# A fused attention and two-stage mixture-of-experts kernel: loads, splits and transposes issued at other places, and GpSimd's two splits of 1024 columns in halves of 512

## The chip, the cores and the metric

The kernel runs on one core of one Trainium2 chip. Its time is the device time of one execution in microseconds (us). The engines are PE (TensorE matmul) with its weight loads PEld, DVE (VectorE), ACT (ScalarE), POOL (GpSimd) and SP (SyncE, which here only issues DMAs). PE has two clock levels, 1.2 and 2.4 GHz; the granted clock in the profile is 0.50 at the lower and 1.00 at the upper one.

## The reference

Three stages follow each other, all in fp32. N = 2176 rows (4 x 512 of xread and 4 x 32 of sread, 17 tiles of 128) are put through both expert stages; D = 512, E = 8 experts, F = 1024.

```
attention(x, state): a = softmax(scale * x @ state.T);  xread = a @ state
                     a2 = softmax(scale * state @ x.T); sread = a2 @ x
                     x1 = concat(xread, sread)                 # heads side by side: 2176 rows of 512
moe1(x): P = exp(x @ w_gate - max)
         for _ in range(8):                                    # the balancing
             P /= P.sum(1) + 1e-9;  P /= P.sum(0) + 1e-9;  P *= N / E
         out = sum over e of P[:, e] * (relu(x @ w1[e]) @ w2[e])
moe2(x): e = argmax(x @ w_gate); each row goes to its one expert e,
         out = gate_w * sigmoid(x @ w_output_gate)[e] * (relu(x @ w1[e]) @ w2[e])
```

## The kernel before, in words

**Precision.** Each fp32 operand of a large product is split into a high part `hi` (a rounded copy, made by ACT) and a rest `lo = x - hi` (made by DVE or POOL); a product is then three matmuls, hi·hi, hi·lo and lo·hi (lines 481 to 483 for the first product of MoE1, 563 to 565 for the second).

**MoE1.** The rows are handled in three passes of six, six and five row tiles (columns 768, 768 and 640 of the transposed input, two halves of 384, 384 and 320 each). A pass has 32 steps, one for each quarter of an expert; the 96 steps are numbered s = 0 to 95. A step first runs `step_mm1(s)`: seven block products instead of eight (operands made of sums of blocks, as Strassen and Winograd do), six matmuls each, in the order 1, 6, 5, 7, 2, 3, 4 (in step 0: 1, 2, 6, 5, 7, 3, 4). Then it runs `step_mm2(s - 1)`: for each row tile of the pass six matmuls of 512 columns. PE's work of step s needs the weights of the step, split and summed; `prep_w1(s + 1)` and `prep_w2(s)` make these during step s: ACT copies the high parts (line 458 `wh`, lines 438, 439, 442), POOL forms four sums (lines 434 to 437, tile `sst`) and the rests: line 459 (`wl`, 1024 columns), 444 (512), 446 (256) and 448 (the rest of the sums, 1024). `rawb` is the one raw buffer for each of the two weights; its next load is issued when the rest is done.

**Order.** The order on every engine is written out by hand. `queue` is a list of small pieces of other work (attention windows, gates, the balancing, the routing), and `pump` takes pieces out of it between products by a credit that grows with PE's time and a price `pace` for each piece. `between(i)` is called after product i of `mm1`, `hooks` and `todo` after a row tile of `step_mm2`. `xsplit(p)` makes the seven split operands of the input of pass p (lines 406 ACT, 408 DVE or POOL).

**Start.** Attention windows 0 and 1 run first, then step 0. In it pieces of the input's sums and splits stand in `early`, and five gates (line 310, eight matmuls of 8 columns for one row tile, tile `psg`) are taken out of the queue. `load_state(b)` clears a tile with DVE (line 142) and has ACT issue four DMAs (line 145); the ones of b = 2 and 3 stand ahead of step 0.

**Balancing.** `sinkhorn()` is a chain of small DVE pieces (lines 336 to 339) and tiny matmuls (line 344, tile `pscol`), run through the queue from step 9 to step 13 (about 262 to 345 us).

**MoE2.** Its first slots (`xT`, `m1`, `hT`, `m2s`: transpose and split the gathered rows, product 1, transpose and split the hidden rows, product 2) start after step 95, together with the end of the routing: `blocks` (lines 1142 on, a DVE chain), `btab` (line 715, 17 matmuls into `ptab`, a table of the rows to gather), `gmul` (line 1198, POOL, tile `osg`) and `gtab` (17 matmuls into `pgat`, the gate of each row). `xT` splits into one pair of buffers `M["xh"]`, `M["xl"]`.

Of the kernel before, what the change touches and what calls it, by code (L numbers as in the profile page):

```python
# [9 lines left out]
F32 = mybir.dt.float32  # L10
# [5 lines left out]
ALU = mybir.AluOpType  # L16
# [5 lines left out]
def tile_state_attention_moe_moe2(  # L22
# [13 lines left out]
    nc = tc.nc  # L36
# [103 lines left out]
    def load_state(b):  # L140
        stp = ap2.tile([P, G, P], F32, tag="stp", name=f"stp{b}")
        nc.vector.memset(stp, 0.0)
        sv = state[b].rearrange("(g q) s d -> q s g d", q=4)
        for q in range(4):
            nc.scalar.dma_start(out=stp[NS * q : NS * (q + 1), :, D * (q % 2) : D * (q % 2) + D], in_=sv[q])
        stps[b] = stp
# [250 lines left out]
    def xsplit(p, t, order=(0, 4, 3, 5, 1, 2, 6)):  # L397
        pool = (3, 1, 6) if p > 0 else ()
        b11, b12, b21, b22, w = xquarters(p)
# [24 lines left out]
    def prep_w1(s):  # L424
# [16 lines left out]
        def f1():  # L441
# [5 lines left out]
                                    in1=wop(s, 0, 2, 1).rearrange(r, k=2).bitcast(F32), op=ALU.subtract)  # L447
            nc.gpsimd.tensor_tensor(out=wop(s, 1, 3, 4), in0=sst.rearrange("p a c -> p (a c)"),  # L448
                                    in1=wop(s, 0, 3, 4).bitcast(F32), op=ALU.subtract)
            if s + 1 < 3 * NU:  # L450
# [3 lines left out]
    def prep_w2(s):  # L454
        raw = rawb[:, 1, :]
        hi = w2p.tile([P, 1024], FR, tag="w2", name=f"wh{s}")
        lo = w2p.tile([P, 1024], FR, tag="w2", name=f"wl{s}")
        nc.scalar.copy(hi, raw)  # L458
        nc.gpsimd.tensor_tensor(out=lo, in0=raw, in1=hi.bitcast(F32), op=ALU.subtract)  # L459
        W2[s] = [a.rearrange("p (k f) -> p k f", k=2) for a in (hi, lo)]  # L460
        if s + 1 < 3 * NU:
            load_raw(s + 1, 1)
# [375 lines left out]
    def xT(sl):  # L838
# [4 lines left out]
        pv = ps.rearrange("p (k t) -> p k t", k=KD)  # L843
        nc.scalar.copy(M["xh"], pv)
        nc.vector.tensor_tensor(out=M["xl"], in0=pv, in1=M["xh"].bitcast(F32), op=ALU.subtract)

    def m1(sl, hooks=()):
        ps2 = [bank(f"pm{sl}_{n}") for n in range(2)]
        hi, lo = M["xh"], M["xl"]
        wh, wl = (wset(sl)[i].rearrange("p (k f) -> p k f", k=KD) for i in (0, 2))  # L850
# [56 lines left out]
    with tc.manual_schedule():  # L907
# [8 lines left out]
        load_x(0, 1)  # L916
        load_raw(0, 0)
        load_x(1, 0, accf[:, 2048:3072])
        load_state(1)
        gate_constants()  # L920
        load_raw(0, 1)
        idle_work(24)
# [26 lines left out]
        C1[2]()  # L949
        C0[3]()  # L950
        sums, T0 = xsums(0, accf)
        parts = xsplit(0, T0, (0, 1, 4, 3, 5, 2, 6))
        parts[0]()
        C1[3]()
        C0[4]()
        C1[4]()
        parts[1]()
        sums[0]()
        sums[1]()
        parts[2]()  # L960

        early = {0: [parts[3], sums[2]], 4: [parts[4]], 1: [parts[5], sums[3]], 2: [parts[6]]}

# [40 lines left out]
        def close_reads():  # L1004
# [5 lines left out]
            smp[0] = rtp[0]  # L1010
            pace[0] = 5.6
            raw2 = ctx.enter_context(tc.tile_pool(name="raw2", bufs=1, side="right", reuse_waits="tile")).tile(
# [10 lines left out]
        def first_rows():  # L1023
            M["xg"] = [xst[:, 512 * i : 512 * i + 512] for i in range(3)]
            M["hs"] = xst[:, 1536:2560].rearrange("p (j t) -> p j t", j=NJ)
            M["y"] = [xst[:, 2560:3072], None]
            M["xh"], M["xl"] = (XR[:, 16384 + 512 * i : 16896 + 512 * i].rearrange("p (k t) -> p k t", k=KD) for i in (0, 1))
            M["hh"], M["hl"] = (HB[:, 1024 * i : 1024 * i + 1024].rearrange("p (j t) -> p j t", j=NJ) for i in (0, 1))
# [7 lines left out]
        def step_mm1(s):  # L1036
            h = PASSES[s // NU][1]
            nxt = prep_w1(s + 1) if s < LAST else [lambda: None] * 2

            def between(i):  # L1040
                if s == 0:
                    for f in early.get(i, ()):
                        f()
                    if i in (0, 4, 1, 2, 3):
                        queue.pop(0)()
                if i == 1:
                    prep_w2(s)
# [38 lines left out]
        queue += [seq(gate([NT - 1]), states_out), close_reads]  # L1086
        pace[0] = 132.0 / (len(queue) - 5)
        credit[0] = -7.3
        balance = sinkhorn()

        for s in range(3 * NU):
# [29 lines left out]
            if p < 2:  # L1121
# [11 lines left out]
            else:  # L1133
# [140 lines left out]
```

## Time and profile before

| what | value |
|---|---|
| median of 3 runs | 1847.14 us (1844.94 to 1849.73) |
| the profiled execution | 1845.63 us, span 1843.4 us |
| PE busy | 1787.8 us, 97% of the span |
| PEld, DVE, ACT, POOL busy | 1594.5, 1219.0, 653.2, 1086.4 us |
| mean granted clock of PE | 0.982 |
| chain that ended last | PE 71%, issue 12%, DVE 8%, DMA 4%, POOL 3%, ACT 1% |

The span is the time from the first to the last instruction that the profile holds; the time of the execution is 2.2 us longer. PE's busy time counts a matmul at the clock that it ran at, so a stretch at half the clock is busy and yet does half the work: what can be gained stands in PE's idle stretches and in the stretches with a granted clock under 1.00.

### The profile page before, as it was taken

What the parts mean: (1) busy time and instruction counts of PE and PEld (TensorE: products, weight loads), DVE (VectorE), ACT (ScalarE), POOL (GpSimd) and SP (SyncE); (2) the same over time, 40 slices, a digit from 0 to 9 for tenths busy, and PEclk for the clock granted to TensorE, in tenths of its full rate; (3) what the DMA queues carried; (4) which work ended last, traced back from release to release, by engine and by line L of the source; (5) the groups of instructions that cost most, each with busy time, mean ns of one, the idle gap of its engine ahead of it and who ended that gap; (6) DMA issues with size and microseconds to landing.
All of it is one profiled execution on the core that took longest, in us unless ns stands there. A gap on an engine that the chain in (4) does not pass through costs nothing.

```text
span 1843.4 us, 25573 instructions
## 1 busy us (share of the span) xinstructions
PE 1787.8 (97%) x9365; PEld 1594.5 (86%) x9365; DVE 1219.0 (66%) x2064; ACT 653.2 (35%) x1114; POOL 1086.4 (59%) x851
## 2 busy tenths in 40 slices
PE   7899998999999999999999999999999999899998
PEld 5889887899999889999999998889999998678886
DVE  5667679976676686666666666897666666545332
ACT  3334332233333433333333333333333334245333
POOL 1445445576776666666667765677787877222212
PEclk8799999999999999999999999999999999899999
DMA  4323421123222322112222222232222222335122
GB/s 108 82 92 81 114 65 55 60 69 101 60 71 68 121 74 68 66 66 65 69 98 69 69 69 92 81 126 81 81 81 81 81 80 81 115 106 195 44 83 91
DMA packets 126619, 154.67 MB, mean 84 GB/s; under 512 B 41424, under 2 KB 91600, under 8 KB 123920
## 3 DMA queue, kind: packets, MB, share of 16 engines
q1 hardware_dynamic: 121920, 142.41, 24.4%
q0 software_dynamic: 3280, 10.23, 1.6%
q8 instruction: 77, 1.26, 0.3%
q14 instruction: 62, 0.51, 0.1%
q10 hardware_dynamic: 1280, 0.26, 0.1%
HBM read 138.99 MB, written 14.42 MB: 83 GB/s over the span
## 4 chain that ended last, share of the span: by engine, by line
PE 71%; issue 12%; DVE 8%; DMA 4%; POOL 3%; ACT 1%; SPq 0%; POOLq 0%; DVEq 0%; ACTq 0%
PE py L563 12%; PE py L564 12%; PE py L565 12%; PE p L481 10%; PE p L483 10%; PE p L482 10%; DMA out_dram<-xst,si 2%; DVE HB L494 1%; DMA out_dram<-y,si 1%; DVE acc L581 1%; POOL XR L448 1%; PE psr L288 1%; PE pss L213 1%; POOL wl L459 1%; PE psg L310 1%
## 5 line engine op out<-in xcount | busy, mean ns | idle before, releaser
L459 POOL TENSOR_TENSOR wl<-rawb,wh 128x1024 fp32r<-128x1024 f32 x96 | 232.0, 2416 | 435.9 <-ACT wh L458 435.8
L481 PE MATMUL p<-XR 128*128 128x384 f32 (+1 forms) x1344 | 448.3, 334 | 9.0 <-ACT u L499 8.7
L483 PE MATMUL p<-XR 128*128 128x384 f32 (+1 forms) x1344 | 444.1, 330 | 9.2 <-POOL XR L448 8.1
L482 PE MATMUL p<-XR 128*128 128x384 f32 (+1 forms) x1344 | 442.7, 329 | 0.0
L563 PE MATMUL py<-wh,HB 128*128 128x512 f32 x1088 | 427.8, 393 | 2.2 <-DVE u L507 2.2
L565 PE MATMUL py<-wh,HB 128*128 128x512 f32 x1088 | 425.2, 391 | 0.0
L564 PE MATMUL py<-wl,HB 128*128 128x512 f32 x1088 | 425.1, 391 | 0.0
L581 DVE SCALAR_TENSOR_TENSOR acc<-py,PG,acc 128x512 f32<-128x512 f32 x461 | 321.2, 740 | 63.3 <-PE py L565 62.6
L448 POOL TENSOR_TENSOR XR<-sst,XR 128x1024 fp32r<-128x1024 f32 x96 | 252.4, 2629 | 56.4 <-ACT XR L442 56.4
L481 PEld LDWEIGHTS p<-XR 128*128 128x128 f32 x1344 | 256.1, 191 | 16.1 <-ACT u L499 8.8
L483 PEld LDWEIGHTS p<-XR 128*128 128x128 f32 x1344 | 255.6, 190 | 11.7 <-POOL XR L448 10.1
L494 DVE SCALAR_TENSOR_TENSOR HB<-u,HB 128x384 fp32r<-128x384 f32 (+1 forms) x192 | 186.7, 974 | 111.5 <-ACT HB L490 111.2
L482 PEld LDWEIGHTS p<-XR 128*128 128x128 f32 x1344 | 256.1, 191 | 3.3
L563 PEld LDWEIGHTS py<-wh,HB 128*128 128x128 f32 x1088 | 204.4, 188 | 44.5 <-DVE u L507 3.0
L565 PEld LDWEIGHTS py<-wh,HB 128*128 128x128 f32 x1088 | 204.2, 188 | 43.4
L564 PEld LDWEIGHTS py<-wl,HB 128*128 128x128 f32 x1088 | 204.4, 188 | 39.0
L499 ACT COPY u<-p 128x384 f32<-128x384 f32 (+1 forms) x96 | 44.3, 461 | 490.3 <-PE p L483 485.1
L444 POOL TENSOR_TENSOR XR<-rawb,XR 128x512 fp32r<-128x512 f32 x96 | 138.9, 1447 | 7.7 <-ACT XR L438 7.7
L442 ACT CAST XR<-sst 128x1024 fp32r<-128x1024 f32 x96 | 100.6, 1048 | 82.6 <-POOL sst L437 82.6
L490 ACT ACTIVATE HB<-u 128x384 fp32r<-128x384 f32 (+1 forms) x192 | 96.9, 505 | 77.9 <-DVE u L526 68.8
L507 DVE TENSOR_TENSOR u<-p,u 128x384 f32<-128x384 f32 (+1 forms) x96 | 51.2, 533 | 97.3 <-PE p L483 96.0
L490 ACT ACTIVATE HB<-p 128x384 fp32r<-128x384 f32 (+1 forms) x96 | 45.5, 474 | 181.6 <-PE p L483 181.6
(296 smaller groups left out, 2491.7 us busy)
## 6 DMA issues: line engine op xcount, KB each, us to landing
rawb<-in_moe_w_dram SPq DMA_DIRECT2D x192, 512.0 KB, 3.5
raw<-in_moe_w_dram SPq DMA_DIRECT2D x15, 1024.0 KB, 6.8
xb<-in_x_dram SPq DMA_DIRECT2D x60, 128.0 KB, 3.4
rawb<-in_moe_w_dram SPq DMA_DIRECT2D x5, 1024.0 KB, 5.0
x1d<-acc SPq DMA_DIRECT2D x16, 256.0 KB, 2.7
xtd<-xtm SPq DMA_DIRECT2D x4, 512.0 KB, 2.8
x1p<-acc SPq DMA_DIRECT2D x8, 256.0 KB, 3.1
xst<-xtd SPq DMA_DIRECT2D x1, 1536.0 KB, 9.5
```

The costliest lines, as they stand in the source:

```text
L444: nc.gpsimd.tensor_tensor(out=wop(s, 1, 0, 2).rearrange(r, k=KD), in0=raw[:, :, 0:P], in1=wop(s, 0, 0, 2).rearrange(r, k=KD).bitcast(F32), ...
L448: nc.gpsimd.tensor_tensor(out=wop(s, 1, 3, 4), in0=sst.rearrange("p a c -> p (a c)"), in1=wop(s, 0, 3, 4).bitcast(F32), op=ALU.subtract)
L459: nc.gpsimd.tensor_tensor(out=lo, in0=raw, in1=hi.bitcast(F32), op=ALU.subtract)
L481: nc.tensor.matmul(ps, wh, xh, start=start and k == 0, stop=False, skip_group_check=True)
L482: nc.tensor.matmul(ps, wh, xl, start=False, stop=False, skip_group_check=True)
L483: nc.tensor.matmul(ps, wl, xh, start=False, stop=stop and k == 1, skip_group_check=True)
L490: nc.scalar.activation(out=hh[:, f, half * h : (half + 1) * h], in_=c, func=AF.Relu)
L494: nc.vector.scalar_tensor_tensor(out=hl[:, f, q], in0=c, scalar=0.0, in1=hh[:, f, q].bitcast(F32), op0=ALU.max, op1=ALU.subtract)
L563: nc.tensor.matmul(ps, hh[:, j, r], whi[:, j, :], start=(j == 0), stop=False)
L564: nc.tensor.matmul(ps, hh[:, j, r], wlo[:, j, :], start=False, stop=False)
L565: nc.tensor.matmul(ps, hl[:, j, r], whi[:, j, :], start=False, stop=(j == 1))
L581: nc.vector.scalar_tensor_tensor(out=a, in0=ps, scalar=PG[:, t, e : e + 1], in1=a, op0=ALU.mult, op1=ALU.add)
```

## The change

All sums, splits, copies and matmuls stay what they were in number and shape, except that two instructions become four. What changes is where they are issued:

- `load_state(2)` and `(3)` are issued by SP instead of ACT. At the start the raw weights and the gate's constants are loaded later than inputs x and states.
- In step 0 the splits and sums are laid out anew, with two of the splits on POOL; eight gates instead of five are taken out of the queue in it, three of them in one place.
- At the end of a pass, `prep_w2` of the next step and `prep_w1` of the one after are issued in the last `step_mm2` of the pass instead of in the first `step_mm1` of the next pass; that step then prepares nothing.
- Lines 448 and 459: POOL's two rests of 1024 columns are two instructions of 512 each.
- `pace` is 5.2 instead of 5.6 in the balancing.
- MoE2: slot 1 gets buffers of its own for its split rows; its transposes and slot 0's are issued between row tiles of the last `step_mm2`; `hT(0)` stands ahead of `blocks`; `btab` stands after the seventh and the second half of the gates' work after the eighth group of `m2s(0)`.

```diff
@@ load_state
-            nc.scalar.dma_start(out=stp[...], in_=sv[q])
+            (nc.scalar if b < 2 else nc.sync).dma_start(out=stp[...], in_=sv[q])
@@ xsplit
-        pool = (3, 1, 6) if p > 0 else ()
+        pool = (3, 1, 6) if p > 0 else (3, 2)
@@ prep_w1, f1
-            nc.gpsimd.tensor_tensor(out=wop(s, 1, 3, 4), in0=sst.rearrange("p a c -> p (a c)"),
-                                    in1=wop(s, 0, 3, 4).bitcast(F32), op=ALU.subtract)
+            for i in (0, 2):
+                nc.gpsimd.tensor_tensor(out=wop(s, 1, 3 + i, 2), in0=sst[:, i : i + 2, :].rearrange("p a c -> p (a c)"),
+                                        in1=wop(s, 0, 3 + i, 2).bitcast(F32), op=ALU.subtract)
@@ prep_w2
-        nc.gpsimd.tensor_tensor(out=lo, in0=raw, in1=hi.bitcast(F32), op=ALU.subtract)
+        for i in range(2):
+            c = slice(512 * i, 512 * i + 512)
+            nc.gpsimd.tensor_tensor(out=lo[:, c], in0=raw[:, c], in1=hi[:, c].bitcast(F32), op=ALU.subtract)
@@ start
-        parts[0]()
-        C1[3]()
-        C0[4]()
-        C1[4]()
-        parts[1]()
-        sums[0]()
-        sums[1]()
-        parts[2]()
-        early = {0: [parts[3], sums[2]], 4: [parts[4]], 1: [parts[5], sums[3]], 2: [parts[6]]}
+        parts[0]()
+        C0[3]()
+        parts[1]()
+        C1[3]()
+        C0[4]()
+        sums[0]()
+        C1[4]()
+        sums[1]()
+        early = {0: [parts[2], parts[3]], 4: [sums[2]], 1: [parts[4], sums[3]], 2: [parts[5], parts[6]]}
...
-            pace[0] = 5.6
+            pace[0] = 5.2
@@ step_mm1
-            nxt = prep_w1(s + 1) if s < LAST else [lambda: None] * 2
+            ahead = s > 0 and s % NU == 0
+            nxt = prep_w1(s + 1) if s < LAST and not ahead else [lambda: None] * 2
-                    if i in (0, 4, 1, 2, 3):
+                    for _ in range((1, 1, 1, 1, 3, 1, 0)[i]):
                         queue.pop(0)()
-                if i == 1:
+                if i == 1 and not ahead:
                     prep_w2(s)
@@ the queue
-        queue += [gate([t]) for t in (6, 7, 0, 1, 2)] + spread(window(2), [3, 4, 5], 4)
+        queue += [gate([t]) for t in (0, 1, 2, 3, 4, 5, 6, 7)] + window(2)
@@ the end of pass 0 and 1
-                step_mm2(s, {ts[2]: [a[0]], ts[3]: [a[1]], ts[4]: [b[0], a[2]], ts[5]: [b[1], a[3]]})
+                w1a, w1b = prep_w1(s + 2)
+                step_mm2(s, {ts[0]: [lambda: prep_w2(s + 1)], ts[1]: [w1a], ts[2]: [a[0]], ts[3]: [a[1], w1b],
+                             ts[4]: [b[0], a[2]], ts[5]: [b[1], a[3]]})
@@ MoE2's start
-                step_mm2(s, {13: [A[12]], 14: [A[13], Bq[12]], 15: [A[14], Bq[13]],
-                             16: [piece[6], Bq[14], A[15], piece[7], lambda: xT(0)]})
+                step_mm2(s, {13: [A[12]], 14: [A[13], Bq[12], lambda: xT(0)], 15: [A[14], Bq[13], piece[6]],
+                             16: [lambda: xT(1), Bq[14], A[15], piece[7]]})
-        xT(1)
-        m1(1, (seq(Rq[4][1], blocks, lambda: load_w(2, 0)), lambda: hT(0)))
-        m2s(0, (None, btab, lambda: gather(2), seq(Rq[3][2], Rq[4][2], gmul)))
+        m1(1, (Rq[4][1], lambda: hT(0), seq(blocks, lambda: load_w(2, 0))))
+        m2s(0, (None,) * 6 + (btab, seq(lambda: gather(2), Rq[3][2], Rq[4][2], gmul)))
```

**ACT at the start of step 0.** `u_103` is the copy of product 1 that PE's next writer of that bank waits for, `stp` a state tile. Before:

```order
L254 COPY xst<-pso_406 128x256
L406 CAST XR<-xst 128x768
L406 CAST XR<-acc 128x768
L145 DMA stp_427<-in_state_dram 32x2x64 x4
L145 DMA stp_433<-in_state_dram 32x2x64 x4
L499 COPY u_103<-p_0_446 128x384
L406 CAST XR<-acc 128x768
```

And after:

```order
L254 COPY xst<-pso_410 128x256
L502 COPY u_103<-p_0_445 128x384
L406 CAST XR<-acc 128x768 x2
L493 ACTIVATE HB<-p_0_445 128x384
L406 CAST XR<-acc 128x768
```

The eight DMA issues and two input splits no longer stand between the last copy of attention and product 1's copy.

**POOL at the end of pass 0.** Lines 434 to 448 (449 after) are `prep_w1`, 459 (462) is `prep_w2`, 408 the split of the next pass's input. Before, up to the first step of the new pass:

```order
L448 TENSOR_TENSOR XR<-sst,XR 128x1024
L408 TENSOR_TENSOR XR<-raw_2243,XR 128x768
L408 TENSOR_TENSOR XR<-xst,XR 128x768
L408 TENSOR_TENSOR XR<-raw_2243,XR 128x768
L459 TENSOR_TENSOR wl_5380<-rawb,wh_5379 128x1024
L434 TENSOR_TENSOR sst<-rawb 128x256
L435 TENSOR_TENSOR sst<-sst,rawb 128x256
L436 TENSOR_TENSOR sst<-rawb 128x256
L437 TENSOR_TENSOR sst<-rawb,sst 128x256
L444 TENSOR_TENSOR XR<-rawb,XR 128x512
L446 TENSOR_TENSOR XR<-rawb,XR 128x256
L448 TENSOR_TENSOR XR<-sst,XR 128x1024
```

And after:

```order
L408 TENSOR_TENSOR XR<-raw_2264,XR 128x768
L462 TENSOR_TENSOR wl_5305<-rawb,wh_5304 128x512 x2
L434 TENSOR_TENSOR sst<-rawb 128x256
L435 TENSOR_TENSOR sst<-sst,rawb 128x256
L436 TENSOR_TENSOR sst<-rawb 128x256
L437 TENSOR_TENSOR sst<-rawb,sst 128x256
L408 TENSOR_TENSOR XR<-xst,XR 128x768
L444 TENSOR_TENSOR XR<-rawb,XR 128x512
L446 TENSOR_TENSOR XR<-rawb,XR 128x256
L449 TENSOR_TENSOR XR<-sst,XR 128x512 x2
L408 TENSOR_TENSOR XR<-raw_2264,XR 128x768
```

The weights' chain has moved ahead of two of the three input splits, out of the first step of the new pass into the last of the old one.

**PE around the two tables of the routing.** `pY` is slot 0's second product, `pt` the transposes of slot 1's hidden rows. Before, with eighteen matmuls `pY` and the eight `pt` between `ptab` and `pgat`:

```order
L880 MATMUL pY_13916<-XR,HB 128x512
L881 MATMUL pY_13916<-XR,HB 128x512
L882 MATMUL pY_13916<-XR,HB 128x512
L715 MATMUL ptab<-osr,ohj_5462 128x24 x8
L715 MATMUL ptab<-osr,ohj_5463 128x24 x8
L715 MATMUL ptab<-osr,ohj_5464 128x24
L880 MATMUL pY_13916<-XR,HB 128x512
```

And after, with the last three:

```order
L718 MATMUL ptab<-osr,ohj_5530 128x24 x2
L718 MATMUL ptab<-osr,ohj_5531 128x24
L884 MATMUL pY_14108<-XR,HB 128x512
L885 MATMUL pY_14108<-XR,HB 128x512
L886 MATMUL pY_14108<-XR,HB 128x512
L873 MATMUL pt_0_14188<-ident,xst 128x128 x4
L873 MATMUL pt_1_14195<-ident,xst 128x128 x4
L718 MATMUL pgat<-osg,ohj_5529 128x48 x8
```

Fifteen matmuls of 512 columns that stood between the two tables now stand ahead of the first.

## Rows read from the trace of the kernel before

**Rows 1.** Windows: start:end us, length, each engine's busy time (instructions), clock, DMA, GB/s.
```profile
42.00:72.00 30.00, 20.23 (x76) 19.91 (x76) 17.54 (x26) 10.51 (x17) 11.45 (x8) 0.60 0.33 84
52.50:67.50 15.00, 15.00 (x59) 15.00 (x58) 9.18 (x16) 5.07 (x8) 9.08 (x7) 0.50 0.22 60
262.00:345.00 83.00, 73.38 (x368) 66.18 (x367) 74.58 (x147) 23.65 (x42) 43.26 (x35) 0.96 0.16 52
645.00:649.00 4.00, 3.39 (x12) 3.39 (x13) 2.79 (x9) 1.90 (x5) 1.10 (x2) 0.67 0.22 76
1154.00:1158.00 4.00, 3.64 (x15) 3.64 (x16) 2.01 (x7) 2.11 (x5) 1.78 (x2) 0.62 0.15 53
1160.00:1260.00 100.00, 94.31 (x528) 83.66 (x527) 91.51 (x184) 34.07 (x64) 69.84 (x57) 1.00 0.31 100
1260.00:1560.00 300.00, 300.00 (x1668) 272.57 (x1668) 200.91 (x348) 112.37 (x207) 237.61 (x185) 1.00 0.26 80
1576.90:1624.00 47.10, 39.16 (x200) 32.32 (x198) 29.35 (x105) 13.94 (x20) 5.81 (x6) 0.89 0.33 118
```

**Rows 2.** Timeline of the start: time, us, engine, instruction [idle before <- releaser].
```profile
46.38 3.71 ACTq L145 DMA_DIRECT2D stp<-in_state_dram  x8
50.13 0.48 ACT L499 COPY u<-p 128x384 f32<-128x384 f32 x1 [5.05 <-DMA stp<-in_state_dram]
50.66 0.69 PE L481 MATMUL p<-XR 128*128 128x384 f32 x1 [8.73 <-ACT u L499]
52.75 1.71 PE L310 MATMUL psg<-wg,xtm 128*128 128x8 f32 x8
55.95 2.35 POOL L459 TENSOR_TENSOR wl<-rawb,wh 128x1024 fp32r<-128x1024 f32 x1 [21.61 <-ACT wh L458]
```

**Rows 3.** Timeline of the balancing: DVE beside POOL, and a wait of PE.
```profile
295.83 0.18 DVE L336 TENSOR_SCALAR sm<-sm 128x17 f32<-128x17 f32 x1
311.79 2.39 POOL L448 TENSOR_TENSOR XR<-sst,XR 128x1024 fp32r<-128x1024 f32 x1 [4.35 <-ACT XR L442]
312.16 2.43 DVE L494 SCALAR_TENSOR_TENSOR HB<-u,HB 128x384 fp32r<-128x384 f32 x1 [0.62 <-ACT HB L490]
317.60 2.33 DVE L336 TENSOR_SCALAR sm<-sm 128x17 f32<-128x17 f32 x1
321.22 0.59 PE L344 MATMUL pscol<-sm,ones 128*128 128x8 f32 x2 [5.20 <-DVE sm L339]
```

**Rows 4.** Timeline of the two changes of pass.
```profile
635.38 2.38 POOL L459 TENSOR_TENSOR wl<-rawb,wh 128x1024 fp32r<-128x1024 f32 x1 [4.67 <-ACT wh L458]
645.61 0.45 PE L483 MATMUL p<-XR 128*128 128x384 f32 x1 [2.14 <-POOL XR L448]
1150.87 0.42 PE L483 MATMUL p<-XR 128*128 128x320 f32 x1 [1.16 <-POOL XR L444]
1154.36 0.41 PE L483 MATMUL p<-XR 128*128 128x320 f32 x1 [2.34 <-POOL XR L448]
```

**Rows 5.** Timeline of MoE2's start.
```profile
1580.69 0.50 PE L855 MATMUL pm<-XR 128*128 128x512 f32 x1 [1.68 <-ACT XR L844]
1593.01 0.50 PE L855 MATMUL pm<-XR 128*128 128x512 f32 x1 [1.32 <-ACT XR L844]
1604.22 0.50 PE L882 MATMUL pY<-XR,HB 128*128 128x512 f32 x1 [3.67 <-DVE HB L873]
1608.69 0.18 DVE L719 TENSOR_SCALAR gi<-ptab 128x24 int32<-128x24 f32 x1 [3.92 <-PE ptab L715]
1613.35 1.71 POOL L1198 TENSOR_TENSOR osg<-sm,gsplit 128x408 fp32r<-128x408 bf16 x2 [3.21 <-DVE gsplit L703]
```

**Rows 6.** POOL's rests: one step of the third pass, and all of line 444.
```profile
1408.63 2.65 POOL L448 TENSOR_TENSOR XR<-sst,XR 128x1024 fp32r<-128x1024 f32 x1
1412.51 0.31 PE L483 MATMUL p<-XR 128*128 128x320 f32 x1
L444 POOL TENSOR_TENSOR XR<-rawb,XR 128x512 fp32r<-128x512 f32 x96 | 138.9, 1447 | 7.7 <-ACT XR L438 7.7
```

More of the change, by code (lines that the diff above doesn't have):

```diff
@@ L144, in load_state @@
         for q in range(4):
-            nc.scalar.dma_start(out=stp[NS * q : NS * (q + 1), :, D * (q % 2) : D * (q % 2) + D], in_=sv[q])
+            (nc.scalar if b < 2 else nc.sync).dma_start(out=stp[NS * q : NS * (q + 1), :, D * (q % 2) : D * (q % 2) + D], in_=sv[q])
         stps[b] = stp
@@ L843, in xT @@
         pv = ps.rearrange("p (k t) -> p k t", k=KD)
-        nc.scalar.copy(M["xh"], pv)
-        nc.vector.tensor_tensor(out=M["xl"], in0=pv, in1=M["xh"].bitcast(F32), op=ALU.subtract)
+        xh, xl = M["x"][sl == 1]
+        nc.scalar.copy(xh, pv)
+        nc.vector.tensor_tensor(out=xl, in0=pv, in1=xh.bitcast(F32), op=ALU.subtract)
     def m1(sl, hooks=()):
         ps2 = [bank(f"pm{sl}_{n}") for n in range(2)]
-        hi, lo = M["xh"], M["xl"]
+        hi, lo = M["x"][sl == 1]
         wh, wl = (wset(sl)[i].rearrange("p (k f) -> p k f", k=KD) for i in (0, 2))
@@ L916, in tile_state_attention_moe_moe2 @@
         load_x(0, 1)
-        load_raw(0, 0)
         load_x(1, 0, accf[:, 2048:3072])
         load_state(1)
-        gate_constants()
-        load_raw(0, 1)
+        load_raw(0, 0)
         idle_work(24)
@@ L927, in tile_state_attention_moe_moe2 @@
         load_x(1, 1)
+        gate_constants()
+        load_raw(0, 1)
         A1[0]()
@@ L949, in tile_state_attention_moe_moe2 @@
         C1[2]()
-        C0[3]()
         sums, T0 = xsums(0, accf)
@@ L1026, in first_rows @@
             M["y"] = [xst[:, 2560:3072], None]
-            M["xh"], M["xl"] = (XR[:, 16384 + 512 * i : 16896 + 512 * i].rearrange("p (k t) -> p k t", k=KD) for i in (0, 1))
+            M["x"] = [[h[:, o + 512 * i : o + 512 * i + 512].rearrange("p (k t) -> p k t", k=KD) for i in (0, 1)]
+                      for h, o in ((XR, 16384), (HB, 2048))]
             M["hh"], M["hl"] = (HB[:, 1024 * i : 1024 * i + 1024].rearrange("p (j t) -> p j t", j=NJ) for i in (0, 1))
@@ L1086, in tile_state_attention_moe_moe2 @@
         queue += [seq(gate([NT - 1]), states_out), close_reads]
-        pace[0] = 132.0 / (len(queue) - 5)
+        pace[0] = 132.0 / (len(queue) - 8)
         credit[0] = -7.3
```

## The prediction

> **What bounds the kernel now.** I read first the page's busy shares (the table above: PE 97%, the chain 71% PE), then windows over the stretches where PE's digit or its granted clock is lower, then each of these in the timeline. In most of the span PE is simply full: the third pass has 300.00 of 300.00 us busy at clock 1.00 [rows 1], so nothing that the change does there can gain. What can be gained lies in six short stretches. In 42 to 72 us PE is busy for 20.23 of 30 us at a mean clock of 0.60; in the balancing (262 to 345) for 73.38 of 83; at each change of pass for less than 4 us at a clock near 0.65; in 1160 to 1260 for 94.31 of 100; and at the start of MoE2 for 39.16 of 47.10 at 0.89 [rows 1]. The reader is to see two losses in each: idle time, and time at half clock that counts as busy.
>
> The sum below is made against the profiled execution's own 1845.63 us, which is 1.5 us under the median of the runs shown.
>
> **A, step 0 (42 to 72 us).** ACT issues the eight state DMAs for 3.71 us and is held by them; its copy of product 1 starts after 5.05 us of idle, and PE's next product after 8.73 us [rows 2]. The change has SP issue them, and the order shows product 1's copy right behind attention's last copy. SP waits for the cleared tile instead; behind it in SP's queue stand only weight loads of later steps, which are not issued before POOL has done step 0's preparation. What is left is work. A mean clock of 0.60 over 30 us means 24 us at the lower level, from about 45.6 to 69.6, with 52.5 to 67.5 wholly in it; of PE's 20.23 us all after 50.66 up to there, 18.9, ran at half and 1.3 at full, so 9.5 + 1.3 = 10.8 us at full clock [rows 1, 2]. Three gates more come in: eight matmuls of 8 columns take 1.71 us at clock 0.50 [rows 2], so 0.86 at full, 2.6 for three; steps 1 to 4 no longer have them, and gain that back. So 13.4 us of work from 42 us on. Before, half clock lasted while products and gates took turns, although PE was then busy without a gap (15.00 of 15 us at 0.50) [rows 1]. I take it that the same alternation, now with three gates in a row, keeps the clock at half until the last gate, which stands ahead of the last product of step 0: 3.6 us of the work at full clock up to 45.6, some 7.4 at half (14.8 us), 2.4 at full, and about 1.6 of small waits on POOL, whose two new input splits stand in its chain. That ends at 64.4 instead of 72.0: 7.6 us, and 2.6 more from the gates, less 1.2 for what I can't see of the re-laid splits: 9 us. Bounds: 4 (half clock to the end of step 1's start, 26.8 us from 42 on, so 72.0 less 68.8 and 2.6 for the gates, less those 1.2 and a little) and 16 (full clock throughout: 42 + 13.4 = 55.4, then some 3 us of waits for POOL's two added splits of 768 columns, which by line 444 [rows 6] are 1.45 x 768/512 = 2.2 us each; 13.4 us and 2.6 for the gates). The later loads of the raw weights cost nothing: POOL idled for 21.61 us before its first weight rest [rows 2], and of that the load takes a few us.
>
> Beside this stands a rule of the Trainium skill (DMA: Bandwidth & Descriptors, section "Issuing engines are not separate DMA queues"): issuing from several engines saves only the sequencer's time to issue, usually small. By it A's idle would shrink by the 3.71 us of issuing alone, and the whole would come out near 1820. The trace disagrees: the wait there was 5.05 us on ACT and 8.73 us on PE, since what was held was ACT's next copy, not a transfer.
>
> **C, the balancing.** Its chain alternates between DVE and PE: PE waits 5.20 us for DVE's small pieces [rows 3]. One of these takes 0.18 us alone and 2.33 us beside a POOL rest of 1024 columns; a DVE rest that starts 0.37 us after such a POOL instruction ends 0.41 us after it, having taken 2.43 us [rows 3]. So DVE stands for as long as POOL's instruction lasts, and with halves it should stand for at most one half: 1.2 us instead of 2.4. That is one half of 2.65 or 2.4 from rows; the nearest row of 512 columns, line 444, means 1.45 us [rows 6], so the gain for each meeting is 0.9 to 1.2 us. DVE is busy for 74.58 of 83 us here [rows 1], so it is on the path. There are two such POOL instructions in each of five steps, and I let three of the ten meetings count: 3.5 us. The pace of 5.2 for 5.6 brings the pieces out sooner: 1.5. C is 5 us; bounds 0 (the DVE chain just waits in the second half) and 9 (all idle but 0.6).
>
> **D and E, the changes of pass.** PE waits 2.14 us for POOL's rest of the sums at 645.61, and 1.16 and 2.34 us at the second change [rows 4], 5.6 in all; the half clock that follows costs 4 x 0.33 + 4 x 0.38 = 2.8 us [rows 1]. With preparations issued a step earlier these go: POOL does the weights before two of the input splits, in time that it idled (4.67 us before one of the rests [rows 4]). The new `wh` copy on ACT must wait for the buffers of two steps before, that is for the last matmul of `step_mm2` just ahead; behind it on ACT stand the other copies of the preparation, nothing that PE needs before the new pass. I take 8 us of 8.4. Bounds 4 (the last input split is late instead, at POOL's 2.4 us per change) and 9.
>
> **F, 1160 to 1260.** Idle 5.7 us, with DVE busy for 91.51 of 100 us [rows 1]. By C's working the halves give DVE back about 1 us per meeting, seven steps long; I take half of the idle time, 3 us; bounds 1 and 5.
>
> **G, the start of MoE2.** PE's waits of 1.68 and 1.32 us for the split of gathered rows and of 3.67 us for `hT(0)`'s rest [rows 5] go, since both splits are made before the last row tiles are done and `hT(0)` stands ahead of DVE's `blocks`: 6.7 us. The clock of 0.89 over 47.1 us [rows 1] means 5.2 us lost to half clock, of which about 4 would go with the waits. Against it stands a new wait. From the end of `ptab` (1608.69) to the end of `osg` (1613.35 + 1.71 = 1615.06) DVE and POOL take 6.4 us [rows 5]; PE had 18 matmuls and the transposes to do meanwhile, and now has three matmuls, at most 0.50 us each [rows 5], and the short transposes: 1.5 us. So PE would stand for 4.9 us before `pgat`, and some 2 us at half clock after it, 1 us lost. 6.7 + 4 - 4.9 - 1 = 5 us; bounds 2 (no half clock goes) and 9 (DVE reaches the gates earlier than the table).
>
> **POOL's halves in steady steps.** Twice two instructions for one each: 2 x 1.25 to 2 x 1.45 us against 2.4 and 2.65 [rows 6], so 0 to 0.7 us more per step. Hidden: POOL is busy for 237.61 of 300 us [rows 1], and the third matmul of the second product, which needs the rest of the sums, starts 1.23 us after it is there (1412.51 against 1408.63 + 2.65) [rows 6]. Since that matmul needs the first half alone, its slack grows. Zero is taken; without that cover 0.7 us in each of 31 steps of the third pass, 22 us, is the worst.
>
> **Sum.** 9 + 5 + 8 + 3 + 5 = 30 us: 1845.6 - 30 = 1815.6. I forecast 1815. The bounds of the terms add up to 11 and 48 us; all at one end at once is unlikely.
>
> **Rivals.**
> Full clock through step 0: A gives 16 instead of 9, maybe less by what then waits on POOL, and the time is 1809. For it: PE has no long idle stretch ahead of step 0's products any more. Against it: 15 us of full busy time at 0.50 [rows 1]. Chance 0.20. The Trainium skill (TensorE: Matmul & The Clock Gate, section "What's actually happening") says that the clock follows how busy PE has been, which is for this case; the trace's 15.00 of 15 us busy at 0.50 disagrees.
> Less relief: DVE's waits are as many as there are POOL instructions, so halves give it twice as many half waits; C is 2, F 1, and one change of pass keeps its wait, D and E 5. 9 + 2 + 5 + 1 + 5 = 22, the time 1823. For it: DVE is busy for 91.51 of 100 us where that matters [rows 1]. Against it: POOL's instructions are as long together. Chance 0.22.
> Slower: POOL's chain becomes the bound of the third pass. If a half costs not 1.3 but well above line 444's 1.45 us [rows 6], say 2.0, the two rests take 8.0 instead of 5.05 us, and POOL's chain outgrows its 62 us of idle time in 300 (2.7 us per step) and the slack of 1.23 us at the second product. It decides from about 2.4 us of growth per step on (30 us of gains over 31 steps, and the slack); at 3.0, and with every gain but C and F kept, the time is 1846 - 22 + 31 x 1.3 = 1864. Against it: no row of 512 columns has a mean near 2.0. Chance 0.04.
> No change (within 0.3%, 5.5 us, about what a measurement of this kernel can tell): step 0 stays on POOL's chain and G's new wait eats G. Time 1843. Chance 0.04.
>
> **How the numbers follow.** The forecast has 0.50, its own range being 1810 to 1820. The range of 1802 to 1828 takes in both rivals on the faster side with the unknown sizes of A and G. Faster by over 0.3% is all but the last two cases: 0.92; within 0.04; slower 0.04.
>
> **What would show it.** In the profile of the changed kernel: ACT's copy of product 1 of step 0 right behind it, with no wait of some 8 us on PE; step 1's second product near 64 us (near 58 with full clock) instead of 72; no wait over 1 us on the sums' rest in the first steps of passes 2 and 3; DVE rests beside POOL of at most 1.4 us; a new wait of 4 to 5 us before `pgat`. Wrong would be: long DVE rests as before, PE not full in the third pass, or idle time of PE that moves to the last input split of a pass.

## The result, and the profile after

The changed kernel takes 1814.75 us (median of 4 runs, 1812.17 to 1817.13) against 1846.74 us for the kernel before on the same chip; the ratio is 0.9825, 95% interval 0.9805 to 0.9845: 32 us or 1.75% faster. The profiled execution took 1815.81 us; its span is 1814.1 us, 29.3 us less than before.

The page of the changed kernel, busy time and the two lines of POOL's halves (line, engine, operation, shape, count; busy us, mean ns; idle before):

```profile
PE 1781.1 (98%) x9365; PEld 1590.6 (88%) x9365; DVE 1205.8 (66%) x2062; ACT 654.4 (36%) x1114; POOL 1123.6 (62%) x1045
L462 POOL TENSOR_TENSOR wl<-rawb,wh 128x512 fp32r<-128x512 f32 x192 | 246.5, 1306 | 404.4 <-ACT wh L459 404.3
L449 POOL TENSOR_TENSOR XR<-sst,XR 128x512 fp32r<-128x512 f32 x192 | 272.8, 1441 | 36.8 <-ACT XR L442 36.8
```

A step now has 2 x 1.306 + 2 x 1.441 = 5.49 us in these instructions. Windows of the changed kernel over the stretches that answer to [rows 1] (columns as there):

```profile
36.70:62.70 26.00, 26.00 (x120) 25.97 (x119) 16.45 (x29) 11.36 (x18) 16.32 (x13) 0.61 0.40 107
44.00:59.00 15.00, 15.00 (x58) 15.00 (x58) 8.30 (x15) 4.88 (x9) 13.16 (x11) 0.50 0.38 104
248.00:331.00 83.00, 76.37 (x369) 68.11 (x368) 72.51 (x146) 23.88 (x42) 46.02 (x44) 0.94 0.18 52
627.00:631.00 4.00, 4.00 (x25) 4.00 (x24) 3.62 (x12) 2.17 (x6) 0.00 (x0) 1.00 0.00 0
1144.00:1150.00 6.00, 3.37 (x14) 3.37 (x14) 5.33 (x21) 1.36 (x3) 1.33 (x2) 0.72 0.25 82
1146.00:1246.00 100.00, 97.63 (x543) 88.33 (x543) 88.34 (x186) 35.95 (x68) 75.21 (x72) 0.98 0.32 100
1244.00:1530.00 286.00, 286.00 (x1589) 259.74 (x1588) 195.02 (x332) 107.62 (x198) 232.97 (x220) 1.00 0.26 80
1551.00:1598.00 47.00, 41.53 (x216) 34.94 (x216) 30.99 (x107) 18.00 (x23) 9.62 (x9) 0.89 0.38 131
```

Step 0 has no idle time left, but most of it still runs at half clock; the first change of pass is gone from the list; the second and the balancing keep idle time and half clock; the third pass is full, as it was. ACT's copy of product 1 marks the start of each step in the timeline. Between these marks the profiled executions took (us, one execution of each kernel; the columns behind the bar are experiments e1, e2, e5, e7 and e8 below):

```
copy of product 1          before  changed   gain  forecast | whole  halves  pace 5.6  count apart  gates ahead
start to step 9 (A)         242.5   228.3    14.2     9     | 228.2   242.2    226.4      230.3       230.2
step 9 to 16 (C)            128.9   128.2     0.7     5     | 130.2   123.3    123.3      127.3       127.3
step 31 to 36 (D)            90.2    86.3     3.8 }   8     |  87.8    89.8     86.3       86.3        86.3
step 63 to 66 (E)            57.5    54.5     3.0 }         |  54.3    56.8     53.7       50.8        54.3
step 66 to 72 (F)            86.4    83.1     3.3     3     |  86.9    82.7     82.8       86.4        83.4
step 95 to the end (G)      288.2   283.9     4.4     5     | 283.8   288.0    283.6      284.3       281.2
```

All other steps took the same to 0.1 us. Parts of identical code differ between the kernels by up to 4 us in A, 1.7 in C, 1.6 in G and 1.1 in F, mostly by the length of their stretches at half clock, so a part is compared below over all kernels that have the code. The gains add up to 29.4 us (29.3 by the spans). The forecast total of 30 us came out, with A 5 us better and C 4 us worse than said.

The lines of the changed kernel that answer to [rows 2, 4, 5] (timeline; a bracket is idle time before the instruction, and what ended it):

```profile
36.74 0.48 ACT L502 COPY u<-p 128x384 f32<-128x384 f32 x1 [0.60 <-PE p L486]
38.48 3.22 PE L310 MATMUL psg<-wg,xst 128*128 128x8 f32 x24
1142.89 3.37 DVE L582 TENSOR_SCALAR acc<-py,PG 128x512 f32<-128x512 f32 x5
1146.63 0.17 PE L675 MATMUL prank<-cum,onesb 128*128 128x8 bf16 x1 [2.76 <-DVE cum L670]
1582.10 3.82 PE L718 MATMUL pgat<-osg,ohj 128*128 128x48 f32 x17 [4.80 <-POOL osg L1206]
```

ACT's copy follows PE's product with no DMA between. At the start of the third pass PE waits for DVE's count, not for POOL any more, and before the gates' table it has the new wait. Before, the wait for the count was shorter, and a gate (eight matmuls of 8 columns) at full clock stood already in the trace (timeline of the kernel before):

```profile
1169.12 0.17 PE L672 MATMUL prank<-cum,onesb 128*128 128x8 bf16 x1 [1.04 <-DVE cum L667]
40.98 0.95 PE L310 MATMUL psg<-wg,xtm 128*128 128x8 f32 x8
```

### The profile page after: what moved, and what is told of

It is laid out like the page before. It is cut to its first block, busy times and chain, and to the rows that moved or that the text cites. A ratio compares the mean times of both kernels' runs of the same rounds, so it can differ in the third digit from the quotient of the medians.

```text
span 1814.1 us, 25784 instructions
## 1 busy us (share of the span) xinstructions
PE 1781.1 (98%) x9365; PEld 1590.6 (88%) x9365; DVE 1205.8 (66%) x2062; ACT 654.4 (36%) x1114; POOL 1123.6 (62%) x1045
## 4 chain that ended last, share of the span: by engine, by line
PE 73%; issue 11%; DVE 7%; DMA 4%; POOL 3%; ACT 1%; SPq 0%; POOLq 0%; DVEq 0%; ACTq 0%
PE py L566 12%; PE py L567 12%; PE py L568 12%; PE p L484 11%; PE p L486 11%; PE p L485 11%; DMA out_dram<-xst,si 2%; DMA out_dram<-y,si 1%; PE psg L310 1%; DVE HB L497 1%; PE psr L288 1%; POOL wl L462 1%; DVE acc L584 1%; PE pss L213 1%; POOL XR L408 1%
## 5 line engine op out<-in xcount | busy, mean ns | idle before, releaser
L462 POOL TENSOR_TENSOR wl<-rawb,wh 128x512 fp32r<-128x512 f32 x192 | 246.5, 1306 | 404.4 <-ACT wh L459 404.3
L449 POOL TENSOR_TENSOR XR<-sst,XR 128x512 fp32r<-128x512 f32 x192 | 272.8, 1441 | 36.8 <-ACT XR L442 36.8
L497 DVE SCALAR_TENSOR_TENSOR HB<-u,HB 128x384 fp32r<-128x384 f32 (+1 forms) x192 | 157.4, 821 | 116.2 <-ACT HB L493 115.9
```

Source lines behind the costliest of these rows:

```text
L449: nc.gpsimd.tensor_tensor(out=wop(s, 1, 3 + i, 2), in0=sst[:, i : i + 2, :].rearrange("p a c -> p (a c)"), in1=wop(s, 0, 3 + i, 2).bitcast ...
L462: nc.gpsimd.tensor_tensor(out=lo[:, c], in0=raw[:, c], in1=hi[:, c].bitcast(F32), op=ALU.subtract)
L497: nc.vector.scalar_tensor_tensor(out=hl[:, f, q], in0=c, scalar=0.0, in1=hh[:, f, q].bitcast(F32), op0=ALU.max, op1=ALU.subtract)
```

## The experiments

All but e2, which edits the kernel before, edit the changed kernel; the edits are shown shortened. The figures in brackets are the ratio of its time to the kernel before and the 95% interval; the changed kernel has 0.9825 (0.9805 to 0.9845).

**e1, the halves taken back** (0.9868, 0.9853 to 0.9884).
```diff
-  for i in (0, 2): tensor_tensor(out=wop(s, 1, 3 + i, 2), ...)      # and the two halves of wl
+  tensor_tensor(out=wop(s, 1, 3, 4), ...)                           # one each of 1024 columns
```


> The changed kernel with POOL's two rests of 1024 columns in one instruction each again, all else as changed. Theory 1 (the forecast's: a DVE instruction stands beside POOL for one POOL instruction, so a half gives half of the wait back, 3.5 us in the balancing and 3 in 1160 to 1260): 6 to 7 us slower than the changed kernel, 1821, and DVE's tiny instructions beside POOL again up to 2.3 us long. Theory 2 (DVE's instructions follow each other without a pause, so the second half meets the next one and the sum of the waits stays): within 2 us of the changed kernel's 1814.75, the balancing (copy of product 1 of step 9 to that of step 15) 112 us as with halves.

Measured 1823.1 us in the median, by the ratios 8 us slower than the changed kernel. In the profiled executions the halves are worth 7.2 us of span: 2.0 in steps 9 to 16, 1.4 in 31 to 36 and 3.8 in 66 to 72. Theory 1 holds for the whole, and its mechanism shows in DVE's longest rest, without and with halves (the instructions of one line, e1 and then the changed kernel; ns min/median/max, first and last start in us):

```profile
L494 DVE SCALAR_TENSOR_TENSOR HB<-u,HB x192: 477/631/2755, 58.5 to 1543.9; 128x384 fp32r<-128x384 f32 x128, 128x320 fp32r<-128x320 f32 x64
L497 DVE SCALAR_TENSOR_TENSOR HB<-u,HB x192: 484/630/1650, 58.8 to 1536.6; 128x384 fp32r<-128x384 f32 x128, 128x320 fp32r<-128x320 f32 x64
```

That DVE's waits are not always cut shows in the balancing's chain of tiny instructions. Timeline of this kernel, without halves, in the seventh of the eight rounds:

```profile
299.80 2.38 POOL L448 TENSOR_TENSOR XR<-sst,XR 128x1024 fp32r<-128x1024 f32 x1 [1.97 <-ACT XR L442]
299.91 2.30 DVE L347 TENSOR_SCALAR sm<-sm 128x8 f32<-128x8 f32 x1
302.25 0.30 DVE L348 TENSOR_TENSOR PG<-PG,sm 128x136 f32<-128x136 f32 x1
```

And of the changed kernel in the same round:

```profile
298.99 2.52 POOL L449 TENSOR_TENSOR XR<-sst,XR 128x512 fp32r<-128x512 f32 x2 [1.29 <-ACT XR L442]
299.40 0.91 DVE L347 TENSOR_SCALAR sm<-sm 128x8 f32<-128x8 f32 x1
300.35 1.33 DVE L348 TENSOR_TENSOR PG<-PG,sm 128x136 f32<-128x136 f32 x1
```

One instruction stood for 2.30 us; now two stand, for 0.91 and 1.33: the pair takes 2.24 instead of 2.60 us. Over the eight rounds, five of which meet POOL's rests, the pair takes 12.4 instead of 14.2 us. So theory 2's mechanism is real in this chain, but it doesn't hold for the larger DVE work of steps 66 to 72.

**e2, the halves alone, in the kernel before** (0.9934, 0.9920 to 0.9947).
```diff
-  tensor_tensor(out=wop(s, 1, 3, 4), ...)                           # one each of 1024 columns
+  for i in (0, 2): tensor_tensor(out=wop(s, 1, 3 + i, 2), ...)      # and the two halves of wl
```


> The kernel before with only the halves. Theory 1: 6 to 7 us faster than before, 1840. Theory 2: within 2 us of before, 1846.

Measured 1836.8 us, 12 us under before: more than either theory said. Steps 9 to 16 give 5.6 us, steps 66 to 72 3.6. A, D, E and G move by 0.3 to 0.7 us each, so what these gain in the changed kernel isn't the halves alone; the other moves behind them were not undone one by one, but for the state loads (e4). Its windows of the balancing and of 1160 to 1260:

```profile
262.00:345.00 83.00, 77.51 (x387) 69.55 (x386) 74.57 (x153) 24.28 (x43) 50.98 (x48) 0.98 0.18 58
1160.00:1260.00 100.00, 96.83 (x549) 87.01 (x548) 88.20 (x187) 35.52 (x67) 75.74 (x73) 1.00 0.33 104
```

PE does 77.51 us of work in the balancing where it did 73.38, and 96.83 where it did 94.31 [rows 1]. The whole change has the halves too, yet gains 0.7 us in steps 9 to 16. So something else in it takes 4 to 5 us back there.

**e3, the old order of the start's loads** (0.9823, 0.9808 to 0.9838).
```diff
+  load_raw(0, 0)                # ahead of load_x(1, 0) and load_state(1), as before
+  gate_constants(); load_raw(0, 1)    # ahead of the first attention window, as before
```


> The changed kernel with the weight and constant loads at the start in their old places. In the changed kernel's trace PE reaches step 0 5.2 us earlier (product 1 ends at 36.7 instead of 41.1), which was in no term of the forecast; there the clock is at half for 6.8 us before step 0 instead of 17.0. Theory 1 (the load order does it: with it inputs arrive earlier, PE does not stand at 9 us and the clock stays up): step 0 begins some 5 us later again, 1820. Rival (the splits and pieces of attention that were laid out anew, or chance in the clock): no change at the start, 1815.

No difference in time (the changed kernel has 0.9825), so the loads' order is worth nothing that can be measured. Its step 0 began late (40.8 us). But so did it in e7 and e8, whose code is that of the changed kernel up to there: 40.4 and 40.3 us instead of 36.7. The window up to step 0 of the changed kernel:

```profile
0.00:36.70 36.70, 29.42 (x179) 22.12 (x179) 21.03 (x40) 16.48 (x30) 7.97 (x14) 0.91 0.44 105
```

And of e8:

```profile
0.00:40.30 40.30, 33.05 (x179) 26.09 (x180) 21.77 (x40) 16.54 (x31) 7.97 (x14) 0.79 0.41 96
```

The same 179 matmuls take 29.42 us at a clock of 0.91, or 33.05 at 0.79. The code is the same up to step 9 in five kernels: e5, e11 and the changed one start step 0 early (36.4 to 36.7 us), e7 and e8 late, and at step 9 they are at 226.4 to 230.3. So the early start isn't due to the code alone. Both executions with the old start (before and e2) were late; whether the change makes early starts more frequent stays open.

**e4, the state loads issued by ACT again** (0.9873, 0.9858 to 0.9888).
```diff
-  (nc.scalar if b < 2 else nc.sync).dma_start(...)
+  nc.scalar.dma_start(...)
```


> The changed kernel with the state DMAs of b = 2 and 3 issued by ACT again. Theory (forecast, term A): ACT is held by them, PE stands for some 8 us before product 2 of step 0, 8 us slower than the changed kernel, 1823. Rival (only the time of issuing counts): 3.7 us slower, 1818.5. Rival 2 (step 0 is bound by POOL's splits and preparation, and the wait is hidden): within 2 us, 1815.

Timeline of the start of step 0 (ACTq is ACT issuing DMAs):

```profile
38.41 4.08 ACTq L145 DMA_DIRECT2D stp<-in_state_dram  x8
42.53 0.48 ACT L502 COPY u<-p 128x384 f32<-128x384 f32 x1 [6.47 <-DMA stp<-in_state_dram]
43.06 0.69 PE L484 MATMUL p<-XR 128*128 128x384 f32 x1 [5.65 <-ACT u L502]
```

The kernel is slower than the changed one by 0.0048 of 1849 us, 8.9 us; by the marks of step 9 it is 8.2. The theory holds: the held ACT is one of the two large parts of the change, about as large as the halves (e1). Issuing from another engine saves only the sequencer's time to issue, by the rule that the forecast weighed (the Trainium skill, DMA: Bandwidth & Descriptors, section "Issuing engines are not separate DMA queues"). Here that time is 4.08 us, ACT is idle for 6.47, and the kernel loses 8 to 9, so the rule doesn't bound the loss in this case.

**e5, pace 5.6 again** (0.9803, 0.9790 to 0.9817).
```diff
-            pace[0] = 5.2
+            pace[0] = 5.6
```


> The changed kernel with pace 5.6 in the balancing again. Steps 9 to 15 took 112.27 us before, 107.77 with the halves alone, 113.55 with everything but the halves and 112.06 with the whole change: so something else in the change costs some 4 us there. Theory (the pace: pieces that come out sooner find DVE not done with the last one, and PE, in order, stands): 107.8 us for these steps, 1810.5 in all. Rival (the pieces meet the steps at another place since the queue before them was laid out anew, whatever the pace): 112 us, 1815.

Steps 9 to 15 take 107.77 us, to a hundredth what they took with the halves alone, and the median is 1811.4. By the ratios that is 4 us faster than the changed kernel, with intervals that still meet; the steps' times settle it. Steps 9 to 16 took 127.3 to 128.7 us in all seven kernels with halves and pace 5.2, and 123.3 to 125.0 in the three with halves and 5.6 in the changed kernel (e5, e10, e11): a mean difference of 3.5 us, at least 2.3. The theory holds. POOL's halves and the DVE chain of one balancing, in e5:

```profile
294.11 2.86 POOL L449 TENSOR_TENSOR XR<-sst,XR 128x512 fp32r<-128x512 f32 x2 [4.35 <-ACT XR L442]
297.96 0.17 DVE L347 TENSOR_SCALAR sm<-sm 128x8 f32<-128x8 f32 x1
298.16 0.30 DVE L348 TENSOR_TENSOR PG<-PG,sm 128x136 f32<-128x136 f32 x1
```

This is the same round as in the rows of e1. Here the chain comes 1 us after POOL's halves have ended and takes 0.17 and 0.30 us; at pace 5.2 it came into them. Over the eight rounds the pair takes 5.9 us at pace 5.6 (e2, e5, e10, e11) and 12.4 at 5.2. PE's waits over 0.6 us in the balancing are two in e5 (0.94 and 3.44), three at 5.2 (1.77, 2.44 and 2.42). In the changed kernel each of the three is followed by half clock, in e5 one. The lengths of these stretches differ for the same code; after the second wait of e5 and of e11 the windows are:

```profile
301.80:305.10 3.30, 3.30 (x12) 3.30 (x11) 2.61 (x7) 0.00 (x0) 3.22 (x5) 0.50 0.42 159
300.90:307.60 6.70, 6.46 (x21) 6.46 (x22) 4.17 (x10) 0.00 (x0) 5.68 (x7) 0.50 0.22 78
```

**e6, seven gates one by one in step 0** (0.9838, 0.9825 to 0.9851).
```diff
-                    for _ in range((1, 1, 1, 1, 3, 1, 0)[i]):
+                    for _ in range((1, 1, 1, 1, 1, 1, 1)[i]):
```


> The changed kernel with seven gates in step 0, one behind each product, instead of eight with three in a row. In the changed kernel the clock falls to half at 40.6 us, in those three gates, and comes back at 61.0, after the last gate. Theory 1 (the forecast's: three in a row lower it): the clock stays at 1.00 through step 0, its start to step 1's copy takes 15 to 18 us instead of 23.5 (POOL's splits then set the end), 5 us faster, 1810. Theory 2 (gates one to one with products lower it all the same): half clock from some product on, 22.5 us or more, 1814 to 1815.

Windows of step 0, and the timeline at PE's wait:

```profile
37.00:47.00 10.00, 9.28 (x64) 8.59 (x64) 9.23 (x16) 6.25 (x10) 4.04 (x3) 1.00 0.65 164
47.00:61.00 14.00, 10.51 (x39) 10.44 (x39) 5.31 (x12) 4.05 (x8) 11.31 (x10) 0.53 0.29 82
```

```profile
44.83 3.92 POOL L462 TENSOR_TENSOR wl<-rawb,wh 128x512 fp32r<-128x512 f32 x2 [2.75 <-ACT wh L459]
48.71 1.80 POOL L408 TENSOR_TENSOR XR<-xst,XR 128x768 fp32r<-128x768 f32 x1
50.56 0.69 PE L485 MATMUL p<-XR 128*128 128x384 f32 x1 [3.49 <-POOL XR L408]
```

The clock stayed at 1.00 for ten us, as theory 1 had it, but PE then overtook POOL: 3.49 us of waiting for a split that stood behind the weights' two halves, and half clock from then on. Step 0's copy to step 1's took 22.8 us, the number of theory 2 and not the 15 to 18 of theory 1. No gain: by the ratios 2.4 us slower than the changed kernel, within the intervals. Ten us of full clock alone were worth nothing here, since POOL's split came next.

**e7, the count of rows apart** (0.9807, 0.9792 to 0.9822).
```diff
-  (fb of routing chunk 1)  matmul(pr[:, 256:264], onesb, cum)     # right behind DVE's count
+  (a piece later)          matmul(bank("ptot")[:, 0:8], onesb, cum)   # the pieces around it are spaced anew
```


> The changed kernel with one matmul of the routing, the total count of rows per expert, issued a piece later and into a bank of its own. In the changed kernel PE stands for 2.76 us before it at 1143.9 (DVE's count is queued behind five products' evictions), and the clock is at half for 3.4 us after it. Theory (that wait ate the rest of what the third pass's start should have given, term E): steps 63 to 66 take 50 to 51 us instead of 54.5, 4 us faster, 1811. Rival (DVE is late itself, and PE then waits at the next thing that DVE owes): under 1.5 us.

The longest wait of PE in its timeline of these steps:

```profile
1151.26 0.41 PE L484 MATMUL p<-XR 128*128 128x320 f32 x1 [1.75 <-DVE acc L582]
```

Steps 63 to 66 fell to 50.8 us as the theory said, but steps 66 to 72 rose from 83.1 to 86.4: of 3.7 us 0.4 stayed. The rival is nearer: DVE, with five evictions of 0.67 us in a row, is late itself, and PE then waits for it elsewhere. By the ratios the two kernels can't be told apart.

**e8, the gates ahead of the row table** (0.9805, 0.9790 to 0.9820).
```diff
-        m2s(0, (None,) * 6 + (btab, seq(lambda: gather(2), Rq[3][2], Rq[4][2], gmul)))
+        m2s(0, (None,) * 6 + (seq(Rq[3][2], Rq[4][2], gmul, btab), lambda: gather(2)))
```


> The changed kernel with DVE's second half of the gates and POOL's table ahead of the routing table of the rows in MoE2's start, not behind it. Theory 1 (PE's wait of 4.80 us before the gates' table is on the path): it falls to about 2.9, and with the half clock that follows (10.2 us) shorter, 2 to 4 us faster, 1811 to 1813. Theory 2 (the weights of the third slot are late anyway: DVE's splits of them end at 1591.7, and PE comes there at 1594.7): the wait before the gates' table falls, a wait at the third slot grows, at most 1 us faster.

Its timeline at the gates' table and at the third slot:

```profile
1581.15 3.63 PE L718 MATMUL pgat<-osg,ohj 128*128 128x48 f32 x17 [2.79 <-POOL osg L1206]
1593.17 0.50 PE L859 MATMUL pm<-HB,XR 128*128 128x512 f32 x1 [0.68 <-ACT XR L848]
```

The wait falls from 4.80 to 2.79 us, and the end of the kernel from step 95 on takes 281.2 instead of 283.9: 2.6 us, theory 1. With the same edit e10 and e11 take 281.2 and 279.6; the other kernels with the changed order take 283.6 to 284.3. The wait at the third slot stays at 0.7.

**e9, step 0's second weights late as well** (0.9819, 0.9801 to 0.9837).
```diff
-                if i == 1 and not ahead:            prep_w2(s)
+                if i == 1 and s > 0 and not ahead:  prep_w2(s)
+                if i == 5 and s == 0:               prep_w2(s)      # with e6's seven gates
```


> The changed kernel with seven gates in step 0, one behind each product (as in the experiment before), and step 0's preparation of the second weights issued after the fifth product instead of after the second product of the order. In that experiment the clock stayed at 1.00 until PE stood for 3.49 us on POOL's second input split, which POOL could start only when its two halves for these weights were done; they took 3.92 us beside DVE. Theory (that one instruction pair ahead of the split is the wait): the wait goes, the clock stays at 1.00 longer, and from step 0's to step 1's copy it takes 17 to 19 us instead of 22.8; 4 us faster than with the seven gates alone, 1811 to 1814. Rival (POOL's chain as a whole, about 16 us with both splits, is the bound of step 0 whatever its order): 22 us or more, PE's wait moves to the sums' rests at the start of step 1.

In this execution step 0's copy to step 1's took 16.8 us, a little under what the theory said, and PE's long wait was gone; the clock stayed at 1.00 until 53.4 us. The next step took 26.2 instead of e6's 21.0 us, with a wait of 1.72 us in it, but it also holds more work: some 25 of PE's matmuls moved up into it from the step behind. Windows of e9's step 0, and of the next step of e9 and e6:

```profile
39.30:53.40 14.10, 12.82 (x90) 12.07 (x89) 13.28 (x21) 6.13 (x11) 8.34 (x7) 1.00 0.49 122
56.10:82.30 26.20, 24.21 (x143) 21.72 (x142) 14.52 (x28) 7.55 (x16) 15.39 (x14) 0.98 0.45 121
59.80:80.80 21.00, 21.00 (x118) 19.22 (x118) 14.09 (x27) 7.57 (x16) 10.66 (x10) 0.96 0.41 101
```

From step 0's copy to step 9's it is 187.7 us against 191.8 in e6, so 4 of the 6 us stayed in this execution. The median is 1814.2, within the interval of the changed kernel, so they don't show in the time.

**e10 and e11, versions from the above.** e11 is e5 and e8 together, e10 has e9's step 0 too.
```diff
 e11:  pace[0] = 5.6;  m2s(0, (None,) * 6 + (seq(Rq[3][2], Rq[4][2], gmul, btab), ...))
 e10:  the same, and the edits of e6 and e9
```


> What the experiments point to, together: the changed kernel with pace 5.6 in the balancing, the gates ahead of the row table in MoE2, seven gates in step 0 and its second weights late. If the parts add up: 4.3 (pace) + 2.6 (gates ahead) + 0 to 4 (step 0): 1804 to 1808 in the median; if MoE2's start or step 0 takes it back, 1810.

> The same without the two edits of step 0: pace 5.6 and the gates ahead of the row table alone. If the parts add up 4.3 + 2.6 = 6.9 us faster than the changed kernel, 1808; if step 0's edits are worth what their theory says, this is 4 us slower than the kernel with all four.

e11: 1806.6 us, 0.9774 (0.9761 to 0.9788), some 9 us faster than the changed kernel by the ratios, where the parts said 6.9. e10: 1807.1, 0.9772 (0.9759 to 0.9786): the edits of step 0 add nothing. The profiled execution of e10, with the code of e9 up to step 1:

```profile
42.00:59.00 17.00, 17.00 (x68) 17.00 (x68) 11.65 (x20) 6.68 (x10) 11.72 (x11) 0.50 0.32 79
```

e9's step 0 ran at 1.00 until 53 us, e10's at 0.50 from 41 on, with the same code, and e10's took 23.5 us to step 1's copy where e9's took 16.8. So single gates don't keep the clock up by themselves, and e6's theory 1 falls. Nor is e9's theory shown: its 16.8 us came with the full clock, and what the later weights are worth without it can't be seen.

## Why the prediction was right or wrong, point by point

**The total** (30 us forecast, 32 by the runs' ratio, 29.3 by the spans) is right, but in part by luck: A came out 5 us better and C 4 us worse than said, and G's sum holds a second pair of errors that cancel.

**A** was forecast at 9 us and is 14.2 in the profiled execution (12.2 to 16.1 in the five with this code). Of the 14.2 us 4.4 come from the start of step 0, whose product 1 ended at 36.7 instead of 41.1 us; the forecast had no term for it, and it is 0.8 to 0.9 in e7 and e8 (e3). From there to step 9 it is 9.7, in e7 and e8 11.3, near the forecast. Right: ACT's hold goes (e4: 8.2 to 8.9 us), and half clock stays to the last gate (15.00 of 15 us busy at 0.50 again). Mis-sized: what steps 1 to 9 give back, forecast as 2.6 us for three gates less 1.2 of doubt about the splits; the marks show 171.9 us before and 167.6 to 168.0 now, so about 4. The gates were priced at half of 1.71, 0.86 us, where the trace of before had 0.95 at full clock, 2.9 for three; where the rest comes from stays open.

**C** failed, by its second step: "The pace of 5.2 for 5.6 brings the pieces out sooner: 1.5." The pace costs some 3.5 us in steps 9 to 16 (e5, e10 and e11 against the seven kernels with 5.2). The first step, 3.5 us for the halves, was too low: at the old pace they give 5.6 (e2; up to 1.7 of it can be a shorter stretch at half clock). At the new one they give 2.0 (e1). There five of eight rounds fall into POOL's halves, where dependent DVE instructions stand one half each.

**D and E**, 8 forecast, 6.8 measured. D is all that was there to get (its idle and half clock are gone). E has less than its share, by a wait that the forecast hadn't looked for: PE's matmul on DVE's count, 1.0 us before and 2.76 now, again with half clock. e7 shows that the wait can't be bought off there alone, since DVE is late. Of D's 3.8 us the halves give 1.4.

**F**, 3 forecast, 3.3 measured, all of it by the halves (86.9 without, 82.7 with them alone). DVE's rests beside POOL were to be 1.4 us at most; the longest in the rows of e1 is 1.65, against 2.76 without halves.

**G**, 5 forecast, 4.4 measured: the old waits went, and the new one was forecast at 4.9 and is 4.80. But 4 us less half clock, less 1 for the new wait, had been forecast too, and none of it came: the mean clock is 0.89 over the 47 us as before. From step 95 to the end (before, then changed) PE's idle time fell from 16.5 to 14.1 us and its busy time by 1.9 us:

```profile
1555.20:1843.40 288.20, 271.67 (x1342) 226.76 (x1340) 118.71 (x209) 111.31 (x135) 66.22 (x48) 0.98 0.30 105
1530.25:1814.10 283.85, 269.79 (x1342) 226.16 (x1340) 119.32 (x210) 111.91 (x135) 66.53 (x49) 0.98 0.30 107
```

So G's size is right in part by luck, and where the 1.9 us come from stays open. What the new wait costs can be had in part (e8).

**POOL's halves in steady steps** cost 0.45 us more per step and no time, as forecast: steps of the third pass are unchanged to 0.01 us. The rival of a slower third pass is refuted.

**The rivals.** Full clock through step 0, by which 1809 was to come out: in the changed kernel it didn't come. In e6 it came for ten us and POOL took it back, so the forecast's own caution about POOL was right. In e9, with later weights, it stayed until 53 us, and up to step 9 that was worth 4.2 us against the same code at half clock (e10: 191.9). Less relief from the halves: right for the balancing at pace 5.2 alone. What stays open is what decides in one execution when the clock falls in step 0; e9 and e10 show that it isn't the code alone.

## What to carry to other kernels

A total that comes out right says little: check each term between marks that both traces have, over several executions where one can take two courses. Here a part that was thrown in as a small gain (a pace) cost most of what another part gave. Halving an instruction that holds another engine up paid in full where that engine's instructions are large (3.8 us in steps 66 to 72); in a chain of short dependent ones it took 0.1 to 0.6 us off a round that met it, and keeping the chain away from it took off up to 1.8. Before a DMA issue is put on a computing engine, look at what stands behind it there: the hold cost 8 to 9 us, and the issuing took 4.

## What the hardware showed that was not expected

The same code can take two courses at half clock: up to step 0, 179 equal matmuls took 29.42 us at a mean clock of 0.91 or 33.05 at 0.79, and in step 0 of e9 and e10 the clock was 1.00 or 0.50. DVE's tiny instruction of 0.17 us stood for 2.30 beside one POOL rest, and with the rest in halves two of them stood, one after the other. POOL can be slow too: two of its halves that take 2.6 us on average took 3.92 in e6, beside a DVE that was busy for 9.23 of 10 us. That DVE is the cause there is not shown.
